# One Trainium2 core, a long convolution beside a feed-forward network: two of the convolution's stages move to unsplit fp32 matmuls on 64-wide parts of the array, the first two weight chunks become classical on centred rows, and VectorE closes every sum

## The chip, the cores and the metric

The kernel runs on one core of a Trainium2 chip. The metric is device time of one execution, in microseconds. PE is TensorE (the 128x128 matmul array), ACT is ScalarE, DVE is VectorE, POOL is GpSimd, SP is the engine that here only issues DMAs. Each engine works through its own list of instructions in order; what another engine produced is waited for by semaphore.

## The reference

Two branches read the same layer-normalized rows `xn` (2048 rows of 576 channels) and are added to the input.

```python
x = A_q
xn = layernorm(x)                                   # over the 576 channels
# A: k_shift = causal 4-tap convolution of k; kv = k_shift * v
#    y = irfft(rfft(kv, 4096) * rfft(ssm_k, 4096))[:2048] + kv * ssm_D    # per channel
#    A = xn * y
# B: h = relu(xn @ w1)      # 576 -> 4608
#    B = h @ w2             # 4608 -> 576
return x + A + B
```

All inputs are fp32. The filter `ssm_k` has 2048 taps per channel.

## The kernel before

**The feed-forward branch.** The 4608 hidden columns are cut into 18 chunks of 256 (`FC`), and the rows into two halves of 1024. One half against one chunk is a *quad* `g`; there are 36 (`QUADS`). A quad first makes its hidden values: 50 matmuls of 512 columns into the two PSUM banks `psh`, by Strassen-Winograd's seven products on sums of weights and of operands (`quad`, `product`). Quad 0 is made the plain way instead, with 56 (`classical`). Then eight *units* of 128 rows (`mm2`) multiply the hidden values by `w2`: 12 matmuls of 288 columns each into a PSUM tile `pso`, of which there are two. Precision is kept by splitting every operand into a high and a low half in the format fp32r and adding three products (high by high, high by low, low by high); ACT makes the high half, DVE or POOL the low one. `matmuls` ties each group of the quads to the one before on PE (`done["pe"]`).

A unit is *closed* in one of two ways. Either DVE adds `pso` to the row sum `acc` (L640). Or, for the units listed in `stage["seeded"]`, ACT copies `acc` into `pso` before the matmuls (L618) and the sum back afterwards (L637).

**The convolution** is a generator, `conv()`, of five stages whose instructions are laid between those of the quads: `later_operands` (rows 1024 to 2047 are normalized and their operands written to DRAM), `fk` (first stage on the filter), `fx` (the short convolution, the gate by `v`, and the first stage on the data), `fm` (second stage, product of the spectra, and second stage back) and `fo` (last stage, gate by `q`, final add). `fx` writes `zx`, `fk` writes `zk`, `fm` reads both and writes `zy`, `fo` reads `zy`; all three are in DRAM, because each stage needs another axis on the partitions.

- `fx`: per row tile, four DVE products by the taps; three of them are added to the sum by an accumulating DMA that POOL issues (L779). `stacks` then splits the tile (L667, L668), writes both halves to DRAM and reads them back stacked as 128 partitions (`xs_n`).
- `fm`: 36 chunks of 512 columns. `second` is three fp32r matmuls of a 128x128 matrix `m_sb` that holds the 64x64 transform twice on its diagonal and zeros elsewhere. Per chunk it runs three times (filter, data, back), with splits by ACT and DVE ahead of each (L840, L841, L871, L872) and a complex product (L905 to L913).
- `fo`: per row tile and half, a split (L952, L953), two matmuls of 288 columns for each of two column ranges, a copy by ACT and an add by DVE (L999, L1000).

**What sets the order.** `tick` is called after each group of quad matmuls with its cost in columns (a quad is some 53,200); it advances the convolution by `rate`, so that the five stages, weighted by the constants `W_...`, end when 97.5% of the feed-forward work is done (`SHARE`). A negative yield (`-PAUSE`) lets that many columns of quad work pass before the next step, to cover a DMA. The matmuls of `fm` and `fo` are not tied by `done["pe"]`: the scheduler places them by its own estimate. `ps_f`, two PSUM banks, serves all the convolution's matmuls.

Weights of quads after the 18th (`kept`) are not split again for the sums of weights `wb` and `wc`: the first 18 quads write them to DRAM and the others load them.

Of the kernel before, what the change touches and what calls it, by code (L numbers as in the profile page):

```python
# [49 lines left out]
START = 40000  # L50
PAUSES = 18
SHARE = 0.975
# [4 lines left out]
N_FK, N_FX, N_FM, N_FO = 4 * T, 4 * T, 3 * NCH, 4 * T  # L57
W_FK, W_FX, W_FM, W_FO = 2.4, 2.9, 3.5, 2.6
KD = 36
KT_GAP = 6000  # L60
N_FB, W_FB = 36, 2.5
FFT_TOTAL = N_FB * W_FB + N_FK * W_FK + N_FX * W_FX + N_FM * W_FM + N_FO * W_FO

OPERANDS = ("00", "01", "s2", "s3", "11", "s1", "s4")
FFN_TOTAL = QUADS * (50 * W_MM + 2 * BT * W_UNIT)
# [13 lines left out]
def transform_constants():  # L79
# [5 lines left out]
    inv = np.zeros((T, A1, 2, U, 2, A1), np.float32)  # L85
    for t in range(T):
        for u in range(U):
            phi = 2 * np.pi * (A2 * p1 + T * u + t) * (f1 - 0.25) / S
            for c, m in enumerate((np.cos(phi), -np.sin(phi))):
                hi, lo = _split12(m)  # L90
                fwd[t, :, :, u, 0, :, c] = hi
                fwd[t, :, :, u, 1, :, c] = lo
                hi, lo = _split12(m.T / S)
                inv[t, :, c, u, u, :] = hi
                inv[t, :, c, u, 1 - u, :] = lo
# [3 lines left out]
    a = np.zeros((GR, 2, A2, 2, GR, A2))  # L99
    for r in range(GR):  # L100
        a[r, :, :, :, r, :] = one
    a = a.reshape(P, P)
    mid = np.stack([*_split12(a), *_split12(a.T)], axis=1)
    return (fwd.reshape(T, P, U, 2, P), inv.reshape(T, P, U, P),
# [4 lines left out]
def h3_ffn_kernel(ctx: ExitStack, tc, x, k, v, shift_k, ssm_k, ssm_D, w1, w2, fwd, inv, mid, out):  # L109
# [25 lines left out]
    parts_n = {kind: dram.tile([NQ, P, 2, 4, P], F32, name=f"{kind}_n") for kind in ("wb", "wc")}  # L135
    xs_n = [dram.tile([U, A1, 2, D], F32, name=f"xs_n{i}") for i in range(2)]
# [43 lines left out]
    def inv_std(t0, n):  # L180

        q = xp.tile([P, 3, BT], F32, tag="q", name=f"q{t0}", bufs=2)[:, :, :n]
# [12 lines left out]
    def normalized_act(dst, src, t):  # L195
        neg = xp.tile([P, 1], F32, tag="neg", name=f"neg{t}", bufs=4)
        nc.vector.scalar_tensor_tensor(neg, mv[:, t, 0:1], -1.0, rstd[:, t:t + 1],
                                       op0=OP.mult, op1=OP.mult)
        return nc.scalar.activation(dst, src, AF.Identity, bias=neg, scale=rstd[:, t:t + 1])

    xo, hl = {}, {}
    done = {}

# [39 lines left out]

    xf = {}

    def first_xT(pool):
# [4 lines left out]
        last = None  # L251
        for t in range(0, BT, 2):
            with tc.issue_after(last.ins) if last else nullcontext():
                for i in range(2):
                    stats(t + i, acc[t + i])
            inv_std(t, 2)
            last = normalized(xn[t], acc[t], t)
            normalized_act(xn[t + 1], acc[t + 1], t + 1)
            for i in range(t, t + 2):
                transposes(ps, xn[i], i)  # L260
                keep_warm(WARM_TILE[i])
            if t == 0:
                split_a(0)
# [3 lines left out]
        with tc.issue_after(last.ins):  # L267
# [3 lines left out]
        with tc.issue_after(high.ins):  # L271
            split_b(0)
            split_d(0)
            split_r(0)
        for o, src in (("00", wide[0]), ("01", wide[1])):
            xf[o] = pool.tile([P, 2, 512], F32, tag=f"xf{o}", name=f"xf{o}")
            nc.scalar.activation(xf[o], src, AF.Copy)

    def second_rows(pool):
        xn = rows_tiles(pool, 1)  # L280
        for t in range(BT, 2 * BT, 2):
            with tc.issue_after(done["low"].ins):
                for i in range(2):
                    stats(t + i, acc[t + i])
            inv_std(t, 2)
            normalized(xn[t % BT], acc[t], t)
            normalized_act(xn[t % BT + 1], acc[t + 1], t + 1)
# [843 lines left out]
```

## Time and profile before

| | |
|---|---|
| median of 3 runs | 1215.97 us (1214.4 to 1220.25) |
| the profiled execution | 1218.57 us, span of its instructions 1216.8 us |
| mean granted PE clock | 0.942 |
| PE busy | 1077.7 us, 89% |
| DVE, ACT, POOL busy | 756.6, 693.9, 451.6 us |
| bytes over DMA | 249.41 MB in 158,615 packets |

The span is the time from the first to the last instruction of the profiled execution. Busy time of PE counts records that overlap, as matmuls are pipelined: a group of matmuls is better costed by how long a run of them takes from the first start to the next group's start. The stages lie in the span as follows, by the first and last instruction of their lines: quads 0 and 1 to 80 us, `later_operands` 81 to 173, `fk` 245 to 395, `fx` 392 to 727, `fm` 730 to 1045, `fo` 1048 to 1211.

### The profile page before, as it was taken

What the parts mean: (1) busy time and instruction counts of PE and PEld (TensorE: products, weight loads), DVE (VectorE), ACT (ScalarE), POOL (GpSimd) and SP (SyncE); (2) the same over time, 40 slices, a digit from 0 to 9 for tenths busy, and PEclk for the clock granted to TensorE, in tenths of its full rate; (3) what the DMA queues carried; (4) which work ended last, traced back from release to release, by engine and by line L of the source; (5) the groups of instructions that cost most, each with busy time, mean ns of one, the idle gap of its engine ahead of it and who ended that gap; (6) DMA issues with size and microseconds to landing.
All of it is one profiled execution on the core that took longest, in us unless ns stands there. A gap on an engine that the chain in (4) does not pass through costs nothing. (4 is left out here: it accounts for less than half of the span.)

```text
span 1216.8 us, 17720 instructions
## 1 busy us (share of the span) xinstructions
PE 1077.7 (89%) x6038; PEld 951.2 (78%) x6038; DVE 756.6 (62%) x1163; ACT 693.9 (57%) x1299; POOL 451.6 (37%) x511
## 2 busy tenths in 40 slices
PE   6888899899999778877979899999999999489996
PEld 3777789789988668766878888888888888378885
DVE  5666664488874365453446546777878776557677
ACT  4545642377878345543523336777777778466663
POOL 3253343444444455443445433333332212123421
PEclk7899999899999989888989999999999999689998
DMA  6278669646555999989999977676666564765555
GB/s 160 70 203 188 225 207 172 132 133 190 186 169 171 240 271 260 254 234 332 341 303 293 289 221 232 192 210 189 191 192 197 175 199 134 219 187 170 172 153 141
DMA packets 158615, 249.41 MB, mean 205 GB/s; under 512 B 70877, under 2 KB 81759, under 8 KB 156732
## 3 DMA queue, kind: packets, MB, share of 16 engines
q1 hardware_dynamic: 130588, 176.53, 48.8%
q0 software_dynamic: 27616, 70.86, 22.9%
q10 hardware_dynamic: 320, 0.88, 0.3%
q8 instruction: 48, 0.79, 0.3%
q14 instruction: 43, 0.35, 0.1%
HBM read 151.74 MB, written 72.88 MB: 185 GB/s over the span
## 5 line engine op out<-in xcount | busy, mean ns | idle before, releaser
L479 PE MATMUL pso<-w,hh 128*128 128x288 f32 x2304 | 488.5, 302 | 17.7 <-ACT acc L637 12.5
L479 PEld LDWEIGHTS pso<-w,hh 128*128 128x128 f32 x2304 | 395.7, 195 | 40.8 <-ACT acc L637 15.0
L479 PE MATMUL pso<-w,ll 128*128 128x288 f32 x1152 | 347.5, 302 | 0.0
L640 DVE TENSOR_TENSOR acc<-pso,acc 128x576 f32<-128x576 f32 x210 | 157.8, 753 | 152.9 <-PE pso L479 138.7
L479 PEld LDWEIGHTS pso<-w,ll 128*128 128x128 f32 x1152 | 223.8, 194 | 1.8
L479 PE MATMUL psh<-x,wa 128*128 128x512 f32 x420 | 117.4, 414 | 27.5 <-ACT psh L545 22.0
L411 POOL TENSOR_TENSOR w<-r,w 128x576 fp32r<-128x576 f32 x72 | 112.2, 1562 | 67.7 <-ACT w L410 67.4
L479 PEld LDWEIGHTS psh<-x,wa 128*128 128x128 f32 x420 | 79.8, 196 | 49.0 <-ACT psh L545 26.1
L479 PE MATMUL psh<-xs,wb 128*128 128x512 f32 x420 | 110.3, 394 | 0.5 <-ACT u L558 0.5
L411 POOL TENSOR_TENSOR wr<-r,wr 128x256 fp32r<-128x256 f32 x36 | 34.6, 962 | 171.4 <-ACT wr L410 164.6
L479 PE MATMUL psh<-hl,wr 128*128 128x512 f32 x280 | 91.8, 407 | 3.4 <-ACT psh L582 2.2
L411 POOL TENSOR_TENSOR wa<-r,wa 128x512 fp32r<-128x512 f32 x36 | 49.6, 1378 | 110.8 <-ACT wa L410 102.9
L479 PEld LDWEIGHTS psh<-xs,wb 128*128 128x128 f32 x420 | 75.6, 189 | 12.5 <-ACT u L558 0.8
L618 ACT ACTIVATE pso<-acc 128x576 f32<-128x576 f32 x78 | 51.0, 654 | 45.9 <-DVE acc L640 44.8
L411 POOL TENSOR_TENSOR wd<-r,wd 128x256 fp32r<-128x256 f32 x36 | 32.1, 893 | 120.9 <-ACT wd L410 120.7
L683 ACT ACTIVATE zx<-psf 128x288 f32<-128x288 f32 x64 | 25.2, 410 | 89.5 <-DMA zx<-zx 47.2
L479 PE MATMUL psh<-xs,wc 128*128 128x512 f32 x210 | 56.6, 406 | 13.2 <-DMA wc<-wc_n 6.7
L637 ACT ACTIVATE acc<-pso 128x576 f32<-128x576 f32 x78 | 50.4, 647 | 30.1 <-PE pso L479 30.1
L779 POOL DMA_DIRECT2D c<-e x48 | 43.7, 917 | 64.4 <-issue 18.3
L660 DVE TENSOR_TENSOR ks<-kt,ks 64x288 fp32r<-64x288 f32 x64 | 53.7, 839 | 19.9 <-ACT ks L659 18.5
L500 DVE SCALAR_TENSOR_TENSOR ll<-psh,hh 128x512 fp32r<-128x512 f32 x70 | 47.9, 684 | 25.1 <-ACT hh L499 25.0
L479 PEld LDWEIGHTS psh<-xs,wc 128*128 128x128 f32 x210 | 39.3, 192 | 24.7 <-DVE ll L500 9.9
(161 smaller groups left out, 2029.2 us busy)
## 6 DMA issues: line engine op xcount, KB each, us to landing
r<-in_w POOLq DMA_DIRECT2D x70, 288.0 KB, 4.9
r<-in_w POOLq DMA_DIRECT2D x35, 512.0 KB, 5.9
c<-e POOLq DMA_DIRECT2D x48, 288.0 KB, 8.0
zk<-zk SPq DMA_DIRECT2D x32, 288.0 KB, 2.9
xs_n<-both SPq DMA_DIRECT2D x16, 576.0 KB, 6.4
xs<-xs_n SPq DMA_DIRECT2D x64, 144.0 KB, 7.1
zx<-zx SPq DMA_DIRECT2D x64, 144.0 KB, 6.4
ztk<-zk SPq DMA_DIRECT2D x36, 256.0 KB, 4.7
```

Source lines behind the costliest of these rows:

```text
L411: nc.gpsimd.tensor_tensor(w[:, 1, :n], src, w[:, 0, :n], OP.subtract)
L479: last = nc.tensor.matmul(ps, a, m, start=start and n == 0, stop=n == len(seq) - 1, skip_group_check=True)
L500: nc.vector.scalar_tensor_tensor(ll, ps, 0.0, hh, op0=OP.max, op1=OP.subtract)
L618: nc.scalar.activation(ps[:, :, :NH], two(acc[t]), AF.Copy)
L637: done["act"] = nc.scalar.activation(two(acc[t]), ps[:, :, :NH], AF.Copy)
L640: done["acc"] = nc.vector.tensor_tensor(two(acc[t]), ps[:, :, :NH], two(acc[t]), OP.add)
L660: nc.vector.tensor_tensor(dst[other], src[own], dst[own], OP.subtract)
L683: nc.scalar.activation(z, ps[:, :NH], AF.Copy)
L779: nc.gpsimd.dma_start(sums[t], e, accum_op=OP.add)
```

## The change

- **fm.** The 36 chunks become 18 pairs. A matmul now multiplies 64 partitions of unsplit fp32 by a 64x64 matrix into 64 PSUM partitions (`turn`): four of them, one for each quarter of the array, handle a pair. The way back is two such rounds, with the matrix and its turned copy, so the complex product needs only four DVE products. The splits, the swap copies and the sums of the complex product are gone. Per pair there are 16 matmuls of 512 columns.
- **fo.** Per row tile, four unsplit fp32 matmuls of 288 columns, from 128 partitions to 64, two side by side in one bank; the gate reads PSUM directly.
- Both stages' matmuls are tied to PE's order (`in_turn`), and the pause between `fm` and `fo` is 28,000 columns where it was 12,000.
- **fx.** The taps are added by DVE, and `stack` splits straight into the other half of the partitions; the accumulating DMAs and the trip through `xs_n` are gone.
- **Closings.** All units are closed by DVE.
- **Start.** The first 512 rows are only centred (DVE and ACT in turn); quads 0 and 1 are classical, the units of those rows multiply by `rstd` while they close, and `scales`, `whole` and `scaled` make the normalized operands for the later quads.
- `wb` and `wc` are split in every quad. The conv's shares and weights are set anew, and parts of `quad` stand in another order (splits and loads between the same units).

```diff
-START = 40000
+PLAIN = 2
-SHARE = 0.975
+SHARE = 0.993
...
-W_FK, W_FX, W_FM, W_FO = 2.4, 2.9, 3.5, 2.6
+W_FK, W_FX, W_FMK, W_FMX, W_FMB, W_FO = 1.5, 2.6, 1.6, 3.2, 2.0, 4.5
...
+    def centre(dst, src, t, how, behind=None):
+        neg = xp.tile([P, 1], F32, tag="neg", name=f"neg{t}", bufs=2)
+        with tc.issue_after(behind.ins) if behind else nullcontext():
+            if how == "dve":
+                stats(t, src)
+                return nc.vector.tensor_scalar(dst, src, mv[:, t, 0:1], None, op0=OP.subtract)
+            nc.scalar.activation(dst, src, AF.Copy, scale=-1.0 / D, accum_out=neg)
+            return nc.scalar.activation(dst, src, AF.Identity, bias=neg)
...
-            inv_std(t, 2)
-            last = normalized(xn[t], acc[t], t)
-            normalized_act(xn[t + 1], acc[t + 1], t + 1)
+            last[t] = centre(xn[t], acc[t], t, ("dve", "act")[t % 2], last.get(t - 2))
...
+    def scales(pool):
+        diag = pool.tile([P, BT, P], F32, tag="diag", name="diag")
+        for i in range(BT):
+            nc.vector.tensor_scalar(diag[:, i, :], ident, rstd[:, i:i + 1], None, op0=OP.mult)
+        nc.tensor.matmul(ps, ones, diag.rearrange("p i n -> p (i n)"), start=True, stop=True)
...
     def split_sums(g, kind, pair):
-        if kept(g):
-            w = wp.tile([P, 2, 4, P], F32R, tag=kind, name=f"{kind}{g}")
-            nc.sync.dma_start(w.bitcast(F32), parts_n[kind][g % NQ])
+        return split_w(g, kind, sums_w[g][:, pair].rearrange("p s c f -> p (s c) f"), (4, P))
...
-        if t in seeded:
-            done["act"] = nc.scalar.activation(two(acc[t]), ps[:, :, :NH], AF.Copy)
+        if g < PLAIN and b == 0:
+            done["acc"] = nc.vector.scalar_tensor_tensor(two(acc[t]), ps[:, :, :NH],
+                                                         rstd[:, t:t + 1], two(acc[t]),
+                                                         op0=OP.mult, op1=OP.add)
         else:
             done["acc"] = nc.vector.tensor_tensor(two(acc[t]), ps[:, :, :NH], two(acc[t]), OP.add)
...
+    def in_turn(ps, a, m, start, stop):
+        with tc.issue_after(done["pe"].ins):
+            done["pe"] = nc.tensor.matmul(ps, a, m, start=start, stop=stop)
...
-                        nc.gpsimd.dma_start(sums[t], e, accum_op=OP.add)
+                        nc.vector.tensor_tensor(sums[t], sums[t], e, OP.add)
...
-                    stks[t, 0], stks[t, 1] = stacks(fp, sums[t], t)
+                    stks[t, u] = fp.tile([P, D], F32R, tag="stk", name=f"xs{t}_{u}", bufs=4)
+                    with here():
+                        stack(stks[t, u], sums[t], u)
...
-            def second(hi, lo, d):
-                ps = fft_psum()
-                seq = [(m_sb[:, d, :], hi), (m_sb[:, d, :], lo), (m_sb[:, d + 1, :], hi)]
+            def turn(banks, terms):
+                for i, (d, src) in enumerate(terms):
+                    for k in range(2):
+                        for r in range(2):
+                            in_turn(banks[k][sides[r ^ k]], m_sb[sides[r], d, :],
+                                    src[sides[r], k, :], i == 0, i == len(terms) - 1)
+            def spectrum(n):
+                banks = [fft_psum() for _ in range(2)]
+                turn(banks, [(0, raw["k", n])])
+                for k in range(2):
+                    for c in range(2):
+                        with here():
+                            nc.scalar.activation(filt[n][c][:, k, :], banks[k], AF.Copy)
+            def product_of(n):
+                banks = [fft_psum() for _ in range(2)]
+                turn(banks, [(0, raw["x", n])])
+                for k in range(2):
+                    for c in range(2):
+                        with here():
+                            nc.vector.tensor_tensor(filt[n][c][:, k, :], banks[k],
+                                                    filt[n][c][:, k, :], OP.mult)
+            def way_back(n):
+                banks = [fft_psum() for _ in range(2)]
+                turn(banks, [(1, filt[n][0]), (2, filt[n][1])])
...
-            yield -0.75 * PAUSE
+            yield -1.75 * PAUSE
...
-                    nc.tensor.matmul(ps[:, :NH], w[:, u, :], hi[:, cols], start=True, stop=False)
-                    nc.tensor.matmul(ps[:, :NH], w[:, u, :], lo[:, cols], start=False, stop=True)
+                    for u in range(U):
+                        in_turn(banks[h][halves(u)[0], :NH], rest_[i][0][:, u, :],
+                                raw[i][u][:, h * NH:(h + 1) * NH], True, True)
```

Three places show how the change moves instructions. In a row stand the line, the operation, what it writes and reads, and its shape; `x4` stands for four in a row. Numbers behind names are buffers.

PE before, where `fm` ends and `fo` begins (`yh`, `yl` and `m_sb` belong to the last way back, `ohi`, `olo` and `wi` to the first row tiles of the last stage):

```order
L849 MATMUL psf<-yh_10274,m_sb 128x512
L849 MATMUL psf<-yl_10273,m_sb 128x512
L849 MATMUL psf<-yh_10274,m_sb 128x512
L997 MATMUL psf<-ohi_10410,wi_10325 128x288 x2
L998 MATMUL psf<-olo_10411,wi_10325 128x288 x2
L997 MATMUL psf<-ohi_10440,wi_10325 128x288
L998 MATMUL psf<-olo_10441,wi_10325 128x288
```

The same place in the change, the first rows and then, further down, the last ones before `fo` (`zo` and `wi`):

```order
L690 MATMUL psf<-k_17_9468,m_sb 64x512 x4
L690 MATMUL psf<-k_17_9469,m_sb 64x512 x4
L495 MATMUL psh_5_9601<-hl_5246,wr_9439 128x512 x2
L495 MATMUL psh_5_9601<-xs_5256,wd_9436 128x512 x6
L495 MATMUL pso_13_9657<-w_9258,hh_1_0_9483 128x288 x2
L495 MATMUL pso_13_9657<-w_9258,ll_1_0_9484 128x288
```

```order
L495 MATMUL pso_10_9831<-w_9652,hh_0_1_9696 128x288 x2
L495 MATMUL pso_10_9831<-w_9652,ll_0_1_9697 128x288
L495 MATMUL psh_2_9805<-xs_5152,wb_9745 128x512 x3
L690 MATMUL psf<-zo_0_9718,wi_9722 64x288
L690 MATMUL psf<-zo_1_9719,wi_9722 64x288
```

Before, no quad matmul stands between the last of `fm` and the first of `fo`; now 35 of 512 columns and 72 of 288 do.

PE in the change, one pair of `fm` (`ztk` is the filter, `ztx` the data, `k_8` the products of pair 8 on their way back):

```order
L690 MATMUL psf<-ztk_8309,m_sb 64x512 x4
L495 MATMUL psh_2_8468<-xs_5152,wb_8376 128x512 x6
L690 MATMUL psf<-ztx_8345,m_sb 64x512 x4
L495 MATMUL psh_5_8603<-xs_5166,wc_8503 128x512 x6
L495 MATMUL pso_11_8546<-w_8234,hh_0_0_8216 128x288 x2
L495 MATMUL pso_11_8546<-w_8234,ll_0_0_8217 128x288
```

Each round of four uses both banks of `ps_f`, so the next round stands behind the reads of the one before; here six quad matmuls lie between them.

DVE in `fx`, before (`e` and `c` are taps, `both` the split, `L640` a closing):

```order
L784 TENSOR_TENSOR c_4447<-c_4447,v_4436 128x576
L778 TENSOR_TENSOR e_1_4713<-k_4553,sk 128x576
L778 TENSOR_TENSOR e_2_4761<-k_4433,sk 128x576
L668 TENSOR_TENSOR both_4602<-c_4447,both_4602 128x576
L640 TENSOR_TENSOR acc_117<-pso_6_5053,acc_117 128x576
L775 TENSOR_TENSOR c_4707<-k_4693,sk 128x576
L592 TENSOR_TENSOR p_15_4914<-psh_2_4780,p_15_4914 128x512
```

and in the change (`L776` adds a tap, `L672` splits, `L652` closes):

```order
L607 TENSOR_TENSOR p_17_5168<-psh_2_5046,p_17_5168 128x512
L652 TENSOR_TENSOR acc_114<-pso_7_5291,acc_114 128x576
L775 TENSOR_TENSOR e_2_5339<-k_4825,sk 128x576
L516 SCALAR_TENSOR_TENSOR ll_1_1_5309<-p_17_5168,hh_1_1_5308 128x512
L776 TENSOR_TENSOR c_5254<-c_5254,e_2_5339 128x576
L516 SCALAR_TENSOR_TENSOR ll_1_0_5358<-psh_4_5259,hh_1_0_5357 128x512
L775 TENSOR_TENSOR e_3_5348<-k_4672,sk 128x576
L776 TENSOR_TENSOR c_5254<-c_5254,e_3_5348 128x576
L652 TENSOR_TENSOR acc_100<-pso_0_5363,acc_100 128x576
```

Each tap now has an add behind it on DVE, and all eight closings of a quad stand among them.

546 lines of the change are left out of this document (247 added, 299 removed).

## The prediction

> **What bounds the kernel now.** I read the page first: the span, the busy shares, the slices.
>
> ```profile
> span 1216.8 us, 17720 instructions
> PE 1077.7 (89%) x6038; PEld 951.2 (78%) x6038; DVE 756.6 (62%) x1163; ACT 693.9 (57%) x1299; POOL 451.6 (37%) x511
> PE   6888899899999778877979899999999999489996
> PEclk7899999899999989888989999999999999689998
> DMA  6278669646555999989999977676666564765555
> ```
>
> PE is the bound, but not everywhere: around slices 13 to 23 its digits fall to 7 and 8 while DMA stands at 9, and slice 34 is a hole. So I cut the span at the stages (columns: us, busy of each engine, granted clock, DMA share, GB/s).
>
> ```profile
> 0.00:57.00 57.00, 43.96 (x187) 31.37 (x188) 35.49 (x84) 26.59 (x47) 13.60 (x20) 0.79 0.38 102
> 57.00:80.00 23.00, 18.87 (x103) 16.02 (x101) 17.18 (x40) 8.88 (x19) 14.57 (x17) 1.00 0.59 183
> 80.00:141.00 61.00, 53.42 (x287) 47.57 (x288) 38.24 (x74) 33.61 (x64) 20.11 (x22) 0.92 0.76 208
> 141.00:252.00 111.00, 102.55 (x595) 91.63 (x594) 58.78 (x85) 44.26 (x82) 48.74 (x53) 0.97 0.80 172
> 252.00:395.00 143.00, 138.94 (x854) 126.99 (x854) 105.14 (x148) 111.54 (x212) 66.08 (x76) 1.00 0.55 176
> 395.00:736.00 341.00, 285.09 (x1589) 255.21 (x1590) 165.22 (x224) 146.27 (x290) 155.41 (x174) 0.92 0.97 276
> 736.00:1040.00 304.00, 294.30 (x1623) 257.46 (x1622) 221.88 (x332) 228.64 (x413) 86.45 (x93) 0.99 0.64 189
> 1040.00:1065.00 25.00, 9.52 (x27) 6.51 (x28) 11.44 (x19) 9.46 (x18) 3.04 (x6) 0.58 0.84 238
> 1065.00:1190.00 125.00, 115.49 (x669) 103.78 (x669) 83.88 (x130) 78.25 (x148) 39.35 (x49) 0.95 0.56 166
> 1190.00:1217.00 27.00, 15.55 (x112) 14.70 (x110) 19.34 (x32) 6.40 (x14) 4.22 (x8) 0.83 0.56 154
> ```
>
> I call *loss* of a stage its idle PE time plus busy time x (1 - clock). `fx` (395 to 736) loses 55.9 + 22.8 = 79 us, the turn to `fo` 15.5 + 4.0 = 19.5, the first 57 us 22, 80 to 252 us 23.5, the stretch after 1065 us 15. `fk` (252 to 395) and `fm` (736 to 1040) lose 4 and 13: there only PE's own work counts. What ends the waits, from the list of PE's waits in `fx` and the timeline at the turn:
>
> ```profile
> PE psf L682 <- DMA xs<-xs_n: 21.2, 7, 8.0
> 1043.78 0.63 PE L849 MATMUL psf<-yh,m_sb 128*128 128x512 f32 x1
> 1051.78 0.85 PE L997 MATMUL psf<-ohi,wi 128*128 128x288 f32 x2 [7.38 <-ACT ohi L952]
> 1062.46 0.85 PE L479 MATMUL pso<-w,hh 128*128 128x288 f32 x2 [0.56 <-ACT pso L618]
> ```
>
> In `fx` PE waits for a round trip through DRAM on a nearly full DMA. At the turn the first matmul of `fo` stands directly behind the last of `fm`, so all quad work queues behind `zy` being written and read back: from 1044 to 1062 us PE does almost nothing.
>
> **What a matmul costs.** Steps are read from the chain, where runs stand back to back.
>
> ```profile
> 1099.77 1.59 PE pso L479 x12
> 1101.36 1.84 PE psh L479 x8
> L849 PE MATMUL psf<-hix,m_sb 128*128 128x512 f32 x72 | 28.8, 399 | 3.5 <-ACT vo L877 3.5
> ```
>
> A step is 1.59/12 = 0.1325 us for 288 columns and 1.84/8 = 0.230 for 512; alone, one lasts 0.399. A quad is 50 x 0.230 + 96 x 0.1325 = 24.2 us of PE.
>
> **fm.** Removed: 36 x 9 = 324 matmuls x 0.230 = 74.5 us. Added: 18 x 16 = 288 of unsplit fp32, 64 wide, which no row shows. A split product adds three of the four products of halves, one step each; an unsplit one owes all four, so I put it at 4 x 0.230 = 0.92 us (estimate from these rows). Below, one step and four tiles at once give 288 x 0.0575 = 17 us; above, 0.92 each in turn gives 265. I take 0.92 for a round of four, 72 x 0.92 = 66 us: the four of a round read, use and write different quarters, so nothing in their operands makes one wait for another. PE's work falls by 8. The Trainium skill, FP8 and Floating Point Precision, section TensorE Precision Notes, says that true FP32 makes four passes through the array, all four products of halves; by it the price of one is the same 0.92 and the sum unchanged.
>
> Each round fills both banks of `ps_f`; the next waits for their readers.
>
> ```profile
> L860 ACT ACTIVATE k<-psf 64x512 f32<-64x512 f32 x72 | 42.5, 590 | 14.1 <-PE psf L849 12.9
> L907 DVE TENSOR_TENSOR k<-psf,k 128x512 f32<-128x512 f32 x36 | 24.8, 688 | 16.8 <-ACT sw L906 15.6 <-PE pso L479 1.0
> ```
>
> Behind the filter's round stand four ACT copies, 4 x 0.59 = 2.4 us; the order puts 1.4 to 3.4 us of quad matmuls there. Behind the data's round stand four DVE products, 2.75 us, with 3.2 to 5.0 us of cover. I book 0.7 us a pair, +13 (0 to +30, should ACT come a queue late). Emptying the array between shapes costs at most 0.399 - 0.230 = 0.17 us on either side of 54 + 16 visits, 24 us; I book 11. The Trainium skill, TensorEngine Tiling (Array Packing), section Key Properties, states that a change of tiling mode drains TensorE; by it the term would be the upper one, 24, and the sum 13 higher. Sum for `fm`: -8 + 13 + 11 = **+16** (-57 to +245 at the bounds).
>
> **fo.** 128 x 0.1325 = 17 us go, 32 side-by-side pairs x 4 x 0.1325 = 17 come: 0 (in turn: +17). The splits and adds fall away; some waits with them, **-4** of 15.
>
> **The turn.** 35 x 0.230 + 72 x 0.1325 = 17.6 us of quad matmuls now stand ahead of `fo`, against the 18 that were lost (1044.4 to 1062.5): **-20** with the clock (-10 to -22).
>
> **fx.** The DRAM trip and 48 accumulating DMAs go; DVE takes their work and the closings.
>
> ```profile
> L775 DVE TENSOR_TENSOR c<-k,sk 128x576 f32<-128x576 f32 x16 | 17.6, 1102 | 6.5 <-DMA k<-in_k 6.3
> L778 DVE TENSOR_TENSOR e<-k,sk 128x576 f32<-128x576 f32 x42 | 35.5, 847 | 13.1 <-DMA c<-e 12.9
> L784 DVE TENSOR_TENSOR c<-c,v 128x576 f32<-128x576 f32 x16 | 13.8, 860 | 10.2 <-DMA c<-e 10.0
> L668 DVE TENSOR_TENSOR both<-c,both 128x576 fp32r<-128x576 f32 x16 | 16.1, 1004 | 7.7 <-ACT both L667 4.8 <-DMA v<-in_v 2.9
> L640 DVE TENSOR_TENSOR acc<-pso,acc 128x576 f32<-128x576 f32 x210 | 157.8, 753 | 152.9 <-PE pso L479 138.7
> L500 DVE SCALAR_TENSOR_TENSOR ll<-psh,hh 128x512 fp32r<-128x512 f32 x70 | 47.9, 684 | 25.1 <-ACT hh L499 25.0
> L423 DVE TENSOR_TENSOR sums<-sums,r 128x256 f32<-128x256 f32 x36 | 17.1, 475 | 0.6
> ```
>
> A row tile costs DVE 1.10 + 3 x 0.85 + 3 x 0.86 + 0.86 + 2 x 1.0 = 9.1 us, 145 for 16. A quad costs it 8 x 0.753 + 6 x 0.69 + 4 x 0.46 = 12.0. In the new order the stage spreads over nine quads: DVE 145 + 9 x 12.0 = 253 us, PE 9 x 24.2 + 128 x 0.1325 = 235. So DVE becomes the bound here, and the loss is at least 18 where it was 79; with waits I say 31: **-48** (-61 at best; -15 if DVE is only 85% busy, 253/0.85 = 298).
>
> **80 to 252 us.** Seeding ends: ACT loses two copies per unit (0.654 and 0.647 below), DVE gains 0.753. PE waited here for ACT. DVE, at 38.2 of the first 61 us, takes up to six closings a quad more, 2.5 x 6 x 0.753 = 11: 49.5 of 61, still below PE. **-8** (-15 to +8).
>
> ```profile
> L618 ACT ACTIVATE pso<-acc 128x576 f32<-128x576 f32 x78 | 51.0, 654 | 45.9 <-DVE acc L640 44.8
> L637 ACT ACTIVATE acc<-pso 128x576 f32<-128x576 f32 x78 | 50.4, 647 | 30.1 <-PE pso L479 30.1
> ```
>
> **Start.** Two rounds of mean, variance, root and inverse stand ahead of the transposes:
>
> ```profile
> 6.09 1.54 DVE L177 BATCH_NORM_STATS2 bn<-acc 128x6 f32<-128x288 f32 x4 [4.95 <-DMA acc<-in_x]
> 18.94 0.42 PE L237 MATMUL psf<-ident,xn 128*64 128x128 f32 x1
> 25.02 3.78 PE L479 MATMUL psh_c<-x,wa 128*128 128x512 f32 x8 [2.47 <-DVE x L218]
> ```
>
> Centring needs per tile on DVE half of that 1.54 and one subtraction, with ACT on every other tile: transposes done near 11, the first full run of matmuls near 17 instead of 25. Some of it returns as quad 1's six more matmuls (+1.4) and one unsplit one (+0.9). **-12** in all (-20 to 0).
>
> **Hidden.** Splitting `wb` and `wc` again in 17 quads:
>
> ```profile
> L410 ACT ACTIVATE wb<-sums 128x512 fp32r<-128x512 f32 x18 | 11.3, 626 | 0.7 <-DVE sums L423 0.7
> L411 POOL TENSOR_TENSOR wb<-sums,wb 128x512 fp32r<-128x512 f32 x18 | 24.9, 1382 | 58.7 <-ACT wb L410 58.7
> ```
>
> 34 x 0.626 = 21 us on ACT and 34 x 1.382 = 47 on POOL, under PE in `fm` and `fo`, where POOL was busy for 86 of 304 us and ACT loses its splits. Without that cover it would be 68.
>
> **The sum.** 16 - 4 - 20 - 48 - 8 - 12 = -76: 1216.8 - 76 = 1141 of span. The median of the runs lay 0.8 below the profiled span, so 1140.
>
> **The rivals.**
>
> *DVE takes what DMA gave up.* For: it stands at 253 against 235 in `fx`, and in order; a closing queued behind taps holds a `pso` tile, and there are two. Then `fx` saves 15 and the stretch from 80 us loses 8: +49, 1189. Against: `fk` ran at 0.97 of PE with DVE and ACT each near 0.75. Chance 0.12.
>
> *Two tiles at a time.* If only two quarters work at once, 144 x 0.92 = 132, +66: 1206. Chance 0.12.
>
> *The halves of a bank take turns (slower).* `turn` sends both row halves of a pair into one bank, one after the other, then the next pair into the other bank. If two row halves cannot write a bank at once, only the second and third of a round overlap: 3 slots instead of 1, and 5 instead of 2 on the way back, 18 x 11 x 0.92 = 182 us, +116: 1256. Nothing in the trace speaks for or against; the destinations are different partitions. The Trainium skill, TensorEngine Tiling (Array Packing), section Gotcha 1: PSUM Pressure, says that different row tiles cannot access the same PSUM bank simultaneously. Chance 0.10.
>
> *No overlap (slower).* Each of a round waits for the one before: 265 instead of 66, +199, and +17 in `fo`: 1356. For: every matmul of the trace has the whole array, so none shows two at once. The point that decides: the other terms save 92, less 24 for waits and drains; 74.5 + 68 = 142 us may be spent on 288 matmuls, so above 1.9 at a time it is faster, below slower. Chance 0.10.
>
> **The numbers.** The forecast has 0.56, with 1100 to 1180 as its own range. The range goes from 1095 (start, turn and `fx` at their best ends, neither waits nor emptying in `fm`) to 1235, which takes in the first two rivals and leaves out 0.2. Less than 0.5% (6 us) cannot be told from no change. Faster: 0.56 + 0.11 + 0.08 = 0.75; slower 0.10 + 0.10 + 0.01 = 0.21; the rest, 0.04, no change.
>
> **What would show it.** In the profile after: a round of four followed by the next matmul after 0.9 to 1.0 us (1.8, 2.8 or 3.7 by the rivals); PE busy at 9 through slice 34; in `fx` DMA well under 0.97 and DVE above 0.9; the first classical run near 12 to 17 us; ACT under 500 us. Wrong it would be if rounds take over 1.9 us, or if DVE's queue holds PE in `fx` for more than 50 us.

## The result, and the profile after

The changed kernel takes 1112.26 us (median of 4 runs, 1111.22 to 1112.83), the kernel before 1217.87 us on the same chip: a ratio of 0.9134, 95% interval 0.9107 to 0.9161. The prediction was 1140, range 1095 to 1235. Faster was right; the gain is 106 us, not 76.

The page of the kernel after: span, busy shares, and rows of its 40 slices.

```profile
span 1109.0 us, 17042 instructions
PE 1057.7 (95%) x6298; PEld 876.2 (79%) x6298; DVE 766.8 (69%) x1136; ACT 478.0 (43%) x914; POOL 470.1 (42%) x504
PE   6898999999999997999999898999999999999998
DVE  3888787457877757999999997444554455456665
DMA  5144854942444447459964332386556654376754
```

PE's digit is now 9 in nearly every slice, and the hole of slice 34 is gone. Below 9 are left only the start, the last slice, and, in slices 15 to 24 where `fx` lies, a 7 and two 8. DMA stood at 9 through most of `fx`; there it now does so in slices 18 and 19 alone, and DVE stands at 9 from slice 16 to 23 instead.

The same span cut at its stages, by windows (columns as before: us, busy of PE, PEld, DVE, ACT, POOL, granted clock, DMA share, GB/s). The rows are the start to quad 2, the rest of the rows up to `fk`, `fk`, `fx`, `fm`, the turn, `fo` and the end.

```profile
0.00:75.00 75.00, 60.61 (x289) 46.21 (x290) 49.41 (x85) 32.80 (x57) 34.92 (x39) 0.91 0.31 82
75.00:267.00 192.00, 185.59 (x1091) 166.24 (x1089) 130.75 (x222) 72.77 (x138) 91.86 (x95) 0.99 0.60 155
267.00:412.00 145.00, 144.49 (x886) 132.09 (x886) 109.84 (x158) 104.07 (x200) 67.58 (x78) 1.00 0.43 138
412.00:715.00 303.00, 278.21 (x1608) 247.80 (x1607) 270.43 (x346) 124.02 (x249) 134.10 (x138) 0.96 0.56 174
715.00:965.00 250.00, 250.00 (x1576) 168.25 (x1575) 121.01 (x196) 110.35 (x210) 79.47 (x84) 1.00 0.58 177
965.00:985.00 20.00, 20.00 (x122) 17.43 (x121) 10.23 (x15) 7.59 (x15) 11.03 (x12) 1.00 0.88 259
985.00:1090.00 105.00, 105.00 (x636) 85.33 (x635) 66.75 (x105) 25.96 (x49) 49.31 (x60) 1.00 0.58 177
1090.00:1109.00 19.00, 13.85 (x103) 12.81 (x101) 8.42 (x13) 0.48 (x1) 1.84 (x4) 0.97 0.60 156
```

Counted as the prediction counts it (a stage's *loss* is its idle PE time, and busy time x (1 - clock)), stage by stage:

| stage | loss before, us | loss after, us | moved | the prediction's term |
|---|---|---|---|---|
| start, to quad 2 | 26.4 (80 us long) | 19.9 (75 us long) | -6.5 | -12, all in all |
| from there to `fk` | 23.4 | 8.3 | -15 | -8 |
| `fk` | 4.1 | 0.5 | -4 | 0 |
| `fx` | 78.7 | 35.9 | -43 | -48 |
| `fm` | 12.6 | 0 | -13 | +13 for waits |
| turn to `fo` | 19.5 | 0 | -19.5 | -20 |
| `fo` and the end | 29.4 | 5.6 | -24 | -4 |

The losses fall by 124 us and the span by 108, so the work of PE at full clock grew by 16 us. About 8 of them can be named: 1 us in `fm` and 2 in `fo`, some 2 us of longer rounds in `fm` (all three below), and the 2.3 us that the prediction booked for the start. The rest is within what this counting can resolve: the clock has two digits, and 0.01 of 1058 us is 10 us.

The timeline of PE in `fm` of the kernel after (start us, us, then the instruction; each unsplit matmul leaves two records, so x8 is a round of four, and x16 are the two rounds of the way back):

```profile
854.07 0.86 PE L495 MATMUL psh<-xs,wd 128*128 128x512 f32 x3
854.85 1.09 PE L690 MATMUL psf<-ztk,m_sb 64*64 64x512 f32 x8
855.87 0.97 PE L495 MATMUL psh<-xs,wd 128*128 128x512 f32 x3
...
863.93 1.95 PE L690 MATMUL psf<-k,m_sb 64*64 64x512 f32 x16
865.81 0.96 PE L495 MATMUL psh<-x,wc 128*128 128x512 f32 x3
```

From the start of a round to the next matmul is 1.02 us, and 1.88 us with a second round behind it. So a further round costs 0.86 us, and a *visit* (one stretch of rounds between quad matmuls) 0.16 more. Ahead of it stand three steps of 0.230, 0.69 us, in 0.78: another 0.09. A pair of chunks is 1.11 + 1.11 + 1.97 = 4.2 us of PE, 18 pairs are 75, where the 324 steps before were 74.5.

What is left in `fx`: the first lines of PE's list of waits, and three groups of DVE, both of the whole execution (the first wait lies wholly in `fx`, the second belongs to the start).

```profile
PE psh L495 <- DVE ll L516: 15.4, 6, 4.2
PE psh_c L495 <- ACT x L208: 7.8, 3, 6.9
```

```profile
L652 DVE TENSOR_TENSOR acc<-pso,acc 128x576 f32<-128x576 f32 x280 | 210.7, 753 | 173.7 <-PE pso L495 172.6
L776 DVE TENSOR_TENSOR c<-c,e 128x576 f32<-128x576 f32 x48 | 55.3, 1152 | 0.5
L775 DVE TENSOR_TENSOR e<-k,sk 128x576 f32<-128x576 f32 x42 | 45.1, 1075 | 0.2
```

In `fx` PE waits for the low halves of hidden values (`ll`) that stand in DVE's queue. The taps (L775) and their adds (L776) are ready as soon as DVE is, 0.2 and 0.5 us of idle time ahead of all of them together. But they take 1.08 and 1.15 us where the closings, of the same size, take 0.753.

### The profile page after: what moved, and what is told of

Same layout as the page of the kernel before. It is cut to its first block, busy times and chain, and to the rows that moved or that the text cites. A ratio compares the mean times of both kernels' runs of the same rounds, so it can differ in the third digit from the quotient of the medians.

```text
span 1109.0 us, 17042 instructions
## 1 busy us (share of the span) xinstructions
PE 1057.7 (95%) x6298; PEld 876.2 (79%) x6298; DVE 766.8 (69%) x1136; ACT 478.0 (43%) x914; POOL 470.1 (42%) x504
## 4 chain that ended last, share of the span: by engine, by line
PE 67%; DVE 19%; issue 5%; DMA 4%; ACT 2%; SPq 1%; POOL 1%; DVEq 0%; POOLq 0%; ACTq 0%
PE pso L495 29%; PE psh L495 26%; PE psf L690 8%; DVE e L775 4%; DVE acc L652 3%; DVE c L776 3%; DVE ll L516 2%; PE psh_c L495 2%; PE psf L678 2%; DMA r<-in_w 1%; DVE xs L672 1%; DVE c L772 1%; DVE c L781 1%; SPq L372 1%; DVE sums L451 1%
## 5 line engine op out<-in xcount | busy, mean ns | idle before, releaser
L495 PE MATMUL pso<-w,hh 128*128 128x288 f32 x2304 | 474.5, 298 | 3.2 <-DVE acc L652 1.6
L495 PEld LDWEIGHTS pso<-w,hh 128*128 128x128 f32 x2304 | 382.5, 189 | 37.1 <-issue 9.0
L495 PE MATMUL pso<-w,ll 128*128 128x288 f32 x1152 | 340.7, 296 | 0.2 <-DVE ll L516 0.2
L652 DVE TENSOR_TENSOR acc<-pso,acc 128x576 f32<-128x576 f32 x280 | 210.7, 753 | 173.7 <-PE pso L495 172.6
L439 POOL TENSOR_TENSOR wb<-sums,wb 128x512 fp32r<-128x512 f32 x34 | 48.1, 1414 | 205.5 <-ACT wb L438 188.8
L495 PE MATMUL psh<-x,wa 128*128 128x512 f32 x408 | 110.2, 404 | 10.1 <-DVE p L607 4.9
L600 ACT ACTIVATE psh<-psh 128x512 f32<-128x512 f32 x34 | 19.9, 585 | 150.8 <-DVE u L598 150.8
L515 ACT ACTIVATE hh<-psh 128x512 fp32r<-128x512 f32 x68 | 40.6, 597 | 84.7 <-PE psh L495 84.5
L672 DVE TENSOR_TENSOR ks<-kt,ks 64x288 fp32r<-64x288 f32 x64 | 54.5, 852 | 18.4 <-ACT ks L671 16.9
L495 PEld LDWEIGHTS psh<-hl,wr 128*128 128x128 f32 x272 | 47.6, 189 | 15.7 <-issue 6.6
L776 DVE TENSOR_TENSOR c<-c,e 128x576 f32<-128x576 f32 x48 | 55.3, 1152 | 0.5
```

What stands on the lines that cost most here:

```text
L439: nc.gpsimd.tensor_tensor(w[:, 1, :n], src, w[:, 0, :n], OP.subtract)
L495: last = nc.tensor.matmul(ps, a, m, start=start and n == 0, stop=n == len(seq) - 1, skip_group_check=True)
L515: done["act"] = nc.scalar.activation(hh, ps, AF.Relu)
L600: nc.scalar.activation(x, y, AF.Copy, scale=-1.0)
L652: done["acc"] = nc.vector.tensor_tensor(two(acc[t]), ps[:, :, :NH], two(acc[t]), OP.add)
L672: nc.vector.tensor_tensor(dst[other], src[own], dst[own], OP.subtract)
```

## The experiments

All were run in three rounds beside the kernel before on the same chip (1217.5 to 1219.6 us in the three groups of four). Ratios are to that kernel. Where two versions are compared, the kernel after has 1112.26 us, 0.9134 (0.9107 to 0.9161).

**Do the four quarters run at once, and does a bank bear two?** In the first, the two banks of a pair use the same two diagonal quarters of the array, so a round is two at a time.

```diff
-                        in_turn(banks[k][sides[r ^ k]], m_sb[sides[r], d, :],
+                        in_turn(banks[k][sides[r]], m_sb[sides[r], d, :],
```

> The changed kernel, but both chunks of a pair use the same two quarters of the array (top left and bottom right), so a round of four matmuls has two pairs that share their quarters. Theory (the overlap comes from four different quarters): the second pair waits for the first, a round takes 2 x 0.92 us instead of 1.0, 72 rounds give +66 us: 1178 us. Rival (neighbouring 64-wide matmuls overlap whatever quarter they use): no change, 1112 us. Rival (the rounds are hidden behind other engines anyway): under +20 us.

Measured 1174.18 us (0.9631, 0.9581 to 0.968): 62 us over the kernel after. The timeline of PE in this run:

```profile
860.17 1.93 PE L690 MATMUL psf<-ztx,m_sb 64*64 64x512 f32 x8
862.03 0.97 PE L495 MATMUL psh<-x,wa 128*128 128x512 f32 x3
...
866.11 3.65 PE L690 MATMUL psf<-k,m_sb 64*64 64x512 f32 x16
869.69 1.65 PE L495 MATMUL psh<-x,wa 128*128 128x512 f32 x6
```

1.86 us instead of 1.02, 3.58 instead of 1.88: each of the 72 rounds has become two, and 72 x 0.86 = 62 us is the whole difference. Four at once is thus shown, and the price of a slot with it.

The next one was meant for another question, whether the tie of `fm` and `fo` to PE's order is what fills the turn. It answered this one.

```diff
     def in_turn(ps, a, m, start, stop):
-        with tc.issue_after(done["pe"].ins):
-            done["pe"] = nc.tensor.matmul(ps, a, m, start=start, stop=stop)
+        nc.tensor.matmul(ps, a, m, start=start, stop=stop)
```

> The kernel after, with the matmuls of `fm` and `fo` no longer tied to the quads' order on PE; the pause of 28,000 columns stays. Theory (the tie is what took the 20 us of the turn away; untied matmuls are laid one directly behind the other and the quads queue behind them): +12 to +22, 1124 to 1134, with an idle stretch of PE of 10 us or more where `fo` begins. Rival (the new stages are short enough in latency that the order does not matter): 1108 to 1116, no hole.

Measured 1189.8 us (0.9779, 0.9731 to 0.9827), 78 us over the kernel after, which neither side had. The timeline of PE:

```profile
871.42 1.08 PE L689 MATMUL psf<-ztk,m_sb 64*64 64x512 f32 x4
872.43 0.40 PE L495 MATMUL pso<-w,ll 128*128 128x288 f32 x1
...
874.19 1.07 PE L689 MATMUL psf<-ztk,m_sb 64*64 64x512 f32 x4
875.20 1.43 PE L495 MATMUL psh<-xs,wb 128*128 128x512 f32 x5
```

Without the tie the scheduler lays quad matmuls between the pair for one bank and the pair for the other. Two matmuls (x4) then take 1.01 us, what four took together. There are 36 visits of 1.11 us more ahead, and on the way back 18 of 1.97: 40 + 35 = 75 of the 78 us. Here the two matmuls of a visit, by the order of `turn`, write the two halves of the partitions of *one* bank, and take the time of one slot. So the rival of the bank's halves falls on this run, as it does on the 1.02 us of a round in the kernel after. The Trainium skill, TensorEngine Tiling (Array Packing), section Gotcha 1: PSUM Pressure, says that different row tiles cannot access the same bank simultaneously; the 1.01 us here, and the 1.02 us of a round with two such pairs, speak against it for tiles that write different partitions.

The hole at the turn that the theory had asked for was not there: the last matmuls of `fm` start at 1061.85 us and the first of `fo` at 1073.57, with quad matmuls between. The next two are on that.

**The turn.** First the kernel after with the old pause between `fm` and `fo`:

```diff
-            yield -1.75 * PAUSE
+            yield -0.75 * PAUSE
```

> The changed kernel with the pause between the second and the last stage back at 12,000 columns; in the order 9.6 us of quad matmuls then stand between the two stages on PE, where the change has 17.6. Theory (the write and the read back of zy take about the 7.4 us that PE waited before, and any quad work tied ahead of them covers it): within 4 us of the change, 1112 to 1116. Rival (the whole 17.6 us is needed): +8 us, 1120, with PE idle ahead of the first matmul of the last stage.

Measured 1111.26 us (0.9126, 0.9078 to 0.9175): no change. 9.6 us of quad matmuls are left between the stages, and they suffice. Then the kernel before with the new pause and with its `fm` and `fo` tied:

```diff
                 for n, (a, m) in enumerate(seq):
-                    nc.tensor.matmul(ps, a, m, start=n == 0, stop=n == 2)
+                    with tc.issue_after(done["pe"].ins) if not n else nullcontext():
+                        last = nc.tensor.matmul(ps, a, m, start=n == 0, stop=n == 2)
+                done["pe"] = last
...
-            yield -0.75 * PAUSE
+            yield -1.75 * PAUSE
```

(The two matmuls of `fo` are tied in the same way.)

> The kernel before with one part of the change alone: the matmuls of the second and last stages are tied to PE's order, and the pause between the two stages is 28,000 columns. 19 us of quad matmuls then stand on PE between the stages. Theory (the hole at the turn was a matter of order alone, worth 20 us): 1198 us, no hole at 1040 us. Rival (the tied order makes the second stage wait for its splits, as PE can no longer pass over a late one): the 20 us are given back there, 1210 to 1225 us.

Measured 1262.08 us (1.0357, 1.0329 to 1.0385): slower than the kernel before by 43 us. Neither side had that: the rival stopped at 1225 us, and looked for the waits inside `fm`. The windows of this run around the end of `fx` and around the turn, and a line of PE's waits:

```profile
590.00:690.00 100.00, 33.87 (x160) 28.08 (x158) 32.67 (x45) 22.95 (x49) 27.57 (x33) 0.61 1.03 296
...
1066.60:1092.00 25.40, 21.94 (x133) 19.59 (x132) 9.95 (x14) 11.31 (x21) 6.92 (x10) 1.00 0.90 262
```

```profile
PE psf L682 <- DMA xs<-xs_n: 85.7, 12, 19.6
```

The turn to `fo` has closed (3.5 us idle of 25.4). In its place PE idles for 66 of 100 us at the turn from `fx` to `fm`, and for most of the time on to `fm`'s first matmul at 706.7 us. From 608 us to there PE runs nothing but the last matmuls of `fx`, which wait for their stacks in a full DMA (share 1.03); the quads are now tied behind `fm`'s first matmul, and that needs all of `fx`. So the quad work between two stages does close a gap, as the prediction said. By this run it does so only where the stage ahead finishes in time, and the kernel before had no such slack in `fx`. Neither the tie alone nor the length of the pause decides in the kernel after: the hole stays away with each of them taken back.

**What held `fx`.** First each of the two DMA uses put back alone. The taps summed by accumulating DMAs (with three buffers of `e`):

```diff
-                        nc.vector.tensor_tensor(sums[t], sums[t], e, OP.add)
+                        nc.gpsimd.dma_start(sums[t], e, accum_op=OP.add)
```

> The changed kernel with the 48 taps of the short convolution added by accumulating DMAs again. Theory (the first stage on the data is bound by DVE, and what made it slow before was the trip of the stacked halves through DRAM): DVE sheds 48 x 1.15 = 55 us, the stage gets 15 to 25 us shorter, 1087 to 1097 us. Rival (the accumulating DMAs themselves were what filled the queues and held the stage before): +15 to +25 us, 1127 to 1137, DMA share back above 0.8 in the stage.

Measured 1114.5 us (0.9149, 0.9109 to 0.919): no change, where both sides expected one. DVE's busy time between 412 and 715 us falls from 270 to 229 us and DMA's share rises from 0.56 to 0.83. PE has 275.5 us of work done in that stretch, against 278.2. A part of what DVE no longer computes it now waits for, in its own queue; the rest was not separated:

```profile
L775 DVE TENSOR_TENSOR e<-k,sk 128x576 f32<-128x576 f32 x42 | 39.4, 941 | 14.0 <-DMA c<-e 13.7
```

(a group of this run: 13.7 us ahead of the taps for the sums of the taps before). Then the stacks' round trip through DRAM:

```diff
-                    stks[t, u] = fp.tile([P, D], F32R, tag="stk", name=f"xs{t}_{u}", bufs=4)
-                    with here():
-                        stack(stks[t, u], sums[t], u)
+                    if u == 0:
+                        stks[t, 0], stks[t, 1] = stacks(fp, sums[t], t)
```

> The changed kernel with the trip of the stacked halves through DRAM put back (one split of 128 partitions, a write, four reads per row tile). Theory (that trip made PE wait before): PE waits for the stacked halves again, some 20 us, DVE and ACT save about 10 us each, +10 to +20 us: 1122 to 1132. Rival (the trip was late only because the accumulating DMAs stood ahead of it): no wait of PE on it, 1102 to 1112.

Measured 1105.59 us (0.9072, 0.9024 to 0.9121): not slower, and whether it is faster is not clear, since the intervals overlap. The theory, that the trip as such costs 10 to 20 us, fell. The time is in the rival's range; PE waits 3.8 us for the stacks in all. Then both at once (with two buffers of `e`, as there is room for no more):

> The kernel after, with both things that `fx` had before put back at once: the taps summed by accumulating DMAs (two buffers of `e`) and the stacks' round trip through DRAM. Each alone cost nothing (1114.5 and 1105.6). Theory (the load on DMA is what held `fx`; either one alone leaves room, both do not): DMA share in `fx` 0.95 or more, PE waits there for `xs` 25 us or more, 1135 to 1160. Rival (what held `fx` before was something else, such as the order of its matmuls): 1104 to 1118 and under 8 us of waits for `xs`.

Measured 1138.83 us (0.9353, 0.9309 to 0.9397): 27 us slower than the kernel after, in the theory's range. The windows of `fx` and `fm`, and the lines of PE's waits:

```profile
412.00:715.00 303.00, 267.97 (x1538) 238.57 (x1537) 195.58 (x271) 107.73 (x221) 164.68 (x181) 0.96 0.96 261
715.00:965.00 250.00, 237.59 (x1477) 162.04 (x1479) 115.28 (x187) 105.15 (x203) 73.03 (x78) 0.97 0.62 191
```

```profile
PE psf L695 <- DMA xs<-xs_n: 17.4, 9, 4.1
PE psf L707 <- DMA m_sb<-in_mid: 9.0, 1, 9.0
```

DMA is at 0.96 again, and PE waits 17.4 us for the stacks (25 had been expected) and 9.0 for a load at the start of `fm`. `fx` lasts longer here, its last matmul ends at 734 us. Each use alone is hidden, both together are not: the load on DMA is what makes the trip long. The two explain 27 of the 43 us that `fx` gained; the rest was not separated.

**What holds `fx` now.** First three of each quad's eight units closed by ACT there, in the way of the kernel before (the last line stands at the head of `fx`, and the other stages have an empty list):

```diff
+        if n in stage["seeded"] and PLAIN <= g < QUADS - 1:
+            seeded.add(t)
+            nc.scalar.activation(ps[:, :, :NH], two(acc[t]), AF.Copy)
...
+        if t in seeded:
+            done["act"] = nc.scalar.activation(two(acc[t]), ps[:, :, :NH], AF.Copy)
+            seeded.remove(t)
...
+            stage["seeded"] = (1, 4, 7)
```

> The changed kernel with three of eight units of a quad closed by ACT (PSUM seeded) in the first stage on the data alone. Theory (DVE is the bound of that stage: 270 of 303 us busy, PE waits for its low halves): DVE sheds 9 x 3 x 0.75 = 20 us there, 1092 to 1102 us. Rival (PE then waits for ACT's seeds and copies as it did before): within 5 us of 1112, with ACT among the waits of PE.

Measured 1095.54 us (0.8995, 0.8972 to 0.9018): 17 us faster than the kernel after, and the fastest version here that computes all of the reference. The window of `fx`:

```profile
412.00:715.00 303.00, 285.30 (x1703) 254.67 (x1701) 248.13 (x326) 166.80 (x323) 139.02 (x145) 0.99 0.60 183
```

PE does 7 us more in the same 303 us at a clock of 0.99 instead of 0.96, and DVE 22 us less. DVE's queue is thus the bound of this stage. Next, its operations take longer than they need to. In this run POOL fills the low halves of weights in quads 15 to 24 with zeros instead of subtracting; it leaves out their part of the result, and is there to measure the time alone:

```diff
+        if 15 <= g <= 24:
+            nc.gpsimd.memset(w[:, 1, :n].bitcast(F32), 0.0)
+        else:
             nc.gpsimd.tensor_tensor(w[:, 1, :n], src, w[:, 0, :n], OP.subtract)
```

> The changed kernel, but in quads 15 to 24 POOL fills the low halves of the weights with zeros instead of subtracting (the products with them are left without effect). It measures what POOL's reading costs DVE. Theory (a DVE operation that reads two SBUF tiles waits while POOL works on SBUF: taps took 1.03 us and their adds 1.15 on average, 0.75 where no POOL subtraction ran beside them): both means fall to 0.75 to 0.85 us, DVE sheds 25 us or more, the kernel 10 to 20: 1092 to 1102 us. Rival (the taps are slow for another reason, their DMAs or the in-place sum): the means stay above 1.0 and the time within 3 us.

Measured 1082.5 us (0.8883, 0.8861 to 0.8905): 30 us faster than the kernel after, where the theory had 10 to 20. Two groups of DVE (the taps and their adds) in this run:

```profile
L779 DVE TENSOR_TENSOR c<-c,e 128x576 f32<-128x576 f32 x48 | 36.1, 753 | 0.5
L778 DVE TENSOR_TENSOR e<-k,sk 128x576 f32<-128x576 f32 x42 | 31.5, 751 | 0.3
```

1152 and 1075 ns have become 753 and 751, the time of a closing: in these two groups 33 us of DVE's 270 in `fx` were time beside POOL's subtractions. That POOL is done sooner is no reason for the gain: in the kernel after PE waits for POOL for 0.6 us in all. Then the old list of six units closed by ACT, in `fx` and in the stretch from 80 us:

```diff
+            stage["seeded"] = (0, 1, 3, 4, 5, 7)
```

> The changed kernel with the closings shared as before (six of eight units by ACT while the later operands are made and in the first stage on the data). Theory (in the first stretch the gain came from ACT being free, in the data's first stage DVE is the bound): 80 to 252 us gives back some 8, the data's first stage gains 15 to 25: 1095 to 1107 us. Rival (closing by DVE alone is better in both): 1115 to 1135 us.

Measured 1103.84 us (0.9052, 0.9031 to 0.9074), in the theory's range. The windows of the two stages:

```profile
75.00:267.00 192.00, 181.94 (x1070) 163.28 (x1069) 114.61 (x202) 90.21 (x169) 87.77 (x93) 0.99 0.60 155
...
412.00:715.00 303.00, 281.90 (x1663) 251.14 (x1661) 220.91 (x292) 196.86 (x376) 139.40 (x145) 0.98 0.59 176
```

In the early stretch PE does 3.7 us less work than in the kernel after: closing by DVE is right there, and worth about that. In `fx` six units by ACT are less good than three, though DVE has 27 us less to do: the two copies of each now hold PE (`pso` waits 10.6 us for ACT in this window).

**The splits that were to be hidden.** The sums of weights and their splits are kept in DRAM again by quads 2 to 17 and loaded by quads 20 to 35:

```diff
+        if kept(g):
+            w = wp.tile([P, 2, 4, P], F32R, tag=kind, name=f"{kind}{g}")
+            nc.sync.dma_start(w.bitcast(F32), parts_n[kind][g % NQ])
...
-        if more:
+        if more and not kept(g + 1):
             sums(g + 1)
```

> The kernel after, with the sums of weights and their splits `wb`, `wc` written to DRAM by the quads 2 to 17 and loaded by the quads 20 to 35, as before: 16 x (1.9 us of sums on DVE, 2 x 1.38 us on POOL, 2 x 0.63 on ACT) go, 16 x 1 MB of loads come. The prediction's step (the new splits are hidden and cost nothing): 1108 to 1114. Rival (in `fx`, quads 20 to 24 lie on DVE, where the sums cost 1.9 us and the subtractions on POOL stretch DVE's own): 1096 to 1105, all of it between 412 and 715 us.

Measured 1102.79 us (0.906, 0.9024 to 0.9097): 9.5 us faster than the kernel after, in the rival's range.

```profile
75.00:267.00 192.00, 183.81 (x1081) 164.98 (x1080) 127.61 (x222) 71.80 (x135) 89.64 (x93) 0.99 0.71 198
...
412.00:715.00 303.00, 287.13 (x1702) 256.06 (x1701) 257.91 (x328) 125.79 (x251) 125.60 (x132) 0.98 0.69 212
```

The gain lies in `fx` (PE 287 for 278, DVE 258 for 270); writing the parts costs 1.8 us of PE's work in the early stretch. At last three of the reliefs together: three units closed by ACT in `fx`, the stacks' trip through DRAM, the kept sums.

> Three reliefs of `fx` together: units 1, 4 and 7 closed by ACT there (1095.5 alone), the stacks' round trip through DRAM (1105.6 alone), the kept sums of weights. If all act on one limit, DVE, and it still stands above PE after the first: the gains add, 1074 to 1086. If the first already brings DVE under PE: 1088 to 1096.

Measured 1119.62 us (0.9217, 0.9164 to 0.927): slower than each of the three alone, and a little slower than the kernel after. Neither side had that.

```profile
412.00:715.00 303.00, 276.39 (x1600) 246.37 (x1600) 213.74 (x275) 142.80 (x279) 119.06 (x127) 0.97 0.86 265
```

```profile
PE psf L714 <- DMA xs<-xs_n: 9.8, 7, 3.3
```

DVE is down to 214 of 303 us, and DMA up to 0.86. PE waits for the stacks again, 9.8 us in this window, and for DVE's closings, 6.3. Two of the three reliefs pay with DMA, and together they bring back a part of the wait that the change had removed. In this window PE does about as much as in the kernel after (276 us at a clock of 0.97, against 278 at 0.96), where each relief alone brought it to 283 to 287 us; some 3 us more are lost ahead of it, as the last matmul of `fk` ends at 409.7 us instead of 406.4. Why closings hold PE with DVE this far below the stage's length is open.

## Why the prediction was right, and where its sum was wrong

The time came out 28 us under the forecast, inside its own range of 1100 to 1180, and each mechanism that it gave for the gain is there. The loss that it gave `fm`, waits for the banks' readers, is not. Its terms, one by one:

- **A round of four.** "0.92 for a round of four" is measured as 0.86, and 0.25 for a visit around it (0.09 ahead and 0.16 behind, each below the forecast's 0.17). 11 us were booked for all 54 + 16 visits; the 54 of `fm` alone take 54 x 0.25 = 13.5, those of `fo` some 2 more. PE's work in `fm` is 75 us, nearly what it was; the prediction had 77. The Trainium skill's four passes (FP8 and Floating Point Precision, section TensorE Precision Notes) fit: 0.86 us is 3.7 of the 0.230 us steps. By the Trainium skill's rule that a change of tiling mode drains TensorE (TensorEngine Tiling (Array Packing), section Key Properties) the term was to be 24; the trace has some 16 us, between the 11 booked and the 24.
- **Waits for the banks' readers: the step that failed most.** "I book 0.7 us a pair, +13" should have been 0, and the 12.6 us that `fm` lost before should have been taken off as well. PE's waits in the kernel before, in `fm` (two lines) and behind 1066 us (one):

```profile
PE psf L849 <- ACT vo L877: 3.5, 3, 1.4
PE psf L849 <- DVE k L907: 3.4, 2, 1.9
...
PE psf L997 <- DVE y L1000: 6.5, 6, 1.8
```

  The matmuls waited for the readers of the banks before the change: these two lines are 6.9 of the 9.7 us of idle time in `fm`. After it `fm` has 250.00 us busy of 250. What is left of such waits lies inside the records: six of the 36 rounds of filter and data take 1.18 to 1.64 us instead of 1.02, some 2 us in all. As the trace reads, the quad matmuls that the order puts behind a round cover the readers, and the fewer visits lie apart; no run tests that. The term is off by 26 us; the span was off by 32 (-76 against -108). That the two lie near each other is chance: `fo` with the end (20 us) and 80 to 252 us (7) also gave more than was booked, and the start, `fx` and the added work of PE took most of that back.
- **`fo` and the end.** "-4 of 15" was -24 of 29. Here too the wait for the banks' readers (6.5 us above) is gone, and the forecast left out what the end loses. Its four matmuls per row tile take 1.12 us to the next matmul and 0.09 ahead, 1.21 a visit: 19 us in all where 17 were booked.
- **The turn.** -20 predicted, -19.5 measured. That quad matmuls stand ahead of `fo` is what closes it; that they do so does not hang on the tie or on the length of the pause alone, as the two runs with each taken back show.
- **`fx`.** -48 predicted, -43 measured, and for the reason given: DMA falls from 0.97 to 0.56 and DVE becomes the bound, at 270 of 303 us (0.89, where the forecast's sign asked for above 0.9). The forecast's "31 with waits" is 36. Its DVE work of 253 us was too low for two reasons: the taps and their adds take 1.08 and 1.15 us, not 0.85 and 0.86, some 23 us more, and the window holds the closings of ten quads (81) instead of nine, 12 us more. Other rows came out cheaper.
- **80 to 252 us.** -8 predicted, -15 measured. Closing by DVE is worth 3.7 of it, not writing the kept parts 1.8. The rest was not tried apart.
- **Start.** -12 predicted, 5 us gained. The transposes end at 11.9 us, near the 11 foreseen, but the first full run of matmuls starts at 21.4, not near 17. The timeline of ACT and then of PE in the kernel after:

```profile
17.20 0.68 ACT L438 ACTIVATE w<-r 128x576 fp32r<-128x576 f32 x1 [4.48 <-DMA r<-in_w]
...
19.76 1.06 ACT L208 ACTIVATE x<-psx 128x512 fp32r<-128x512 f32 x2
```

```profile
20.39 0.80 PE L495 MATMUL psh_c<-x,wa 128*128 128x512 f32 x1 [6.87 <-ACT x L208]
21.37 3.78 PE L495 MATMUL psh_c<-x,wa 128*128 128x512 f32 x8 [0.18 <-DVE x L209]
```

  On ACT's queue the second half of the operand's splits stands behind splits of weights, the first of which waits 4.48 us for its load. The prediction looked at what stands ahead of the transposes and not at the queue behind them. This is read from the trace; no run moved it.
- **Hidden.** "34 x 0.626 us on ACT and 47 us on POOL, under PE" holds in `fm` and `fo` and not in `fx`: keeping the parts gives 9.5 us. The prediction had the 4 sums of a quad in DVE's 12.0 us, but this step gave them no price, nor did it count that POOL's subtractions stretch DVE's work.

The rivals of two at a time, of a bank's halves in turn and of no overlap fell on the length of a round, and the two runs that force two at a time (+62 and +78) show what it would have cost. The first rival, DVE taking what DMA gave up, is half true: it is the bound of `fx` now, at a price of 36 us and not of 64. The prediction's "every matmul of the trace has the whole array" overlooks the transposes of 128x64, one of which it shows; that one stands alone, so the argument stays.

## What to carry to other kernels

Before booking a wait for a buffer's readers, see in the order how much other work stands between two visits of the buffer, and see whether the old form has such a wait that now goes. Matmuls that use quarters of the array saved time here only where they stood side by side in PE's order, so tie them. And weigh a relief by the engine that pays for it: three that do good or no harm alone can lose together when two of them pay with the same DMA.

## What the runs showed of the hardware

DVE operations with both sources in SBUF slow down beside POOL's subtractions; those that read PSUM do not. Taking the kernel after's instructions one by one, taps and adds that no subtraction of POOL overlaps take about 0.75 us, and those overlapped for the whole of their time 1.46 (10 taps) and 1.83 (4 adds) on average; closings take 0.75 in both cases. The timelines of DVE and then of POOL in `fx`:

```profile
501.73 1.75 DVE L776 TENSOR_TENSOR c<-c,e 128x576 f32<-128x576 f32 x1
...
514.47 1.82 DVE L516 SCALAR_TENSOR_TENSOR ll<-u,hh 128x512 fp32r<-128x512 f32 x1
```

```profile
501.56 1.30 POOL L439 TENSOR_TENSOR wa<-r,wa 128x512 fp32r<-128x512 f32 x1
...
514.46 1.28 POOL L439 TENSOR_TENSOR wb<-sums,wb 128x512 fp32r<-128x512 f32 x1 [1.44 <-ACT wb L438]
```

Each DVE operation starts just behind one of POOL's (501.73 after 501.56, 514.47 after 514.46) and ends 0.62 and 0.55 us after it (503.48 after 502.86, 516.29 after 515.74), a little less than its own duration alone later (0.75 and 0.68): it looks as if it stood still until POOL was done. The Trainium skill, SBUF — State Buffer, section SBUF: two separate sides, says that a DVE operation with two SBUF inputs and a GpSimd operation that reads SBUF lock each other out for a whole instruction. These rows agree, and so does the run in which POOL fills instead of reading (751 and 753 ns).
